# Attention with block sums and a squared-ReLU layer on one core: x moved by 128 bytes, the sums of w_out's blocks held back, and other constants in the planner

## Chip, cores and metric

The kernel runs on one core of a Trainium2 chip. The metric is the device time of one execution in microseconds (us). Four engines compute: TensorE (PE in the profile; PEld is its loading of stationary operands), VectorE (DVE), ScalarE (ACT) and GpSimd (POOL). SyncE (SP) issues every DMA of this kernel.

## The reference

```python
k_sum = k.reshape(B, H, nb, block, D).max(axis=3)      # B=4, H=8, S=768, D=64, block=32
v_sum = v.reshape(B, H, nb, block, D).mean(axis=3)
scores_l = scale * q @ k.T            # kept where |i - j| < 16
scores_s = scale * q @ k_sum.T + log(block)
a = softmax(concat([scores_l masked, scores_s]))
attn = a @ concat([v, v_sum])
x = attn as [3072 tokens, 512]
h = x @ w_in                          # [512, 2048]
g = relu(h) ** 2
out = g @ w_out                       # [2048, 512]
```

All of it is float32. TensorE multiplies it in a split form: each operand is taken as a high and a low part, and three products (high by high, low by high, high by low) are added.

## The kernel before

**Work.** The attention goes in 48 groups of 64 queries, the layer in units of 512 tokens, each unit in 16 items (a block of 128 columns of w_in, and the 128 rows of w_out that go with it). `xh` and `xl` hold the high and the low part of x for two units at a time. A first matmul of an item (`hidden`, line 1018 in the first two units, line 1305 in the others) is 12 matmuls of 512 columns: for each of four blocks of 128 inputs, w high with xh, w low with xh and w high with xl, all added in one bank of PSUM. A second one (line 1042) has 12 matmuls with w_out as the moving operand. In the four later units the second product is formed with fewer multiplications, from sums and differences of blocks of w_out (`combine`) and of g (`products`, line 1419: six matmuls each, gh or gl moving), and a part of the last two units' first products likewise from sums of x (`mixed`, line 1610; its x operands lie in `xh`, `xl`, in the room of `kb`, as xkb, and in tiles xs, xa, xgh, xgl).

**Order.** The order on each engine isn't written out. Every step is a task with an engine, a cost, a key (its due time), the tasks that it comes after and the buffers that it takes and uses; `Plan.order` plays the tasks through with those costs and writes the instructions in the order that comes out. Where several tasks of an engine are ready, the smallest key goes first; `begin` is a time ahead of which a task isn't started, `behind` a task that must have been started, `late` time added to a DMA's landing. A DMA lands, for the planner, its bytes at 350 GB/s and 1.9 us after its issue. A first matmul group costs 2.73 us there, a second one 12 times 0.2268 us.

**Buffers.** Tile `t` has three slots of 4,096 bytes. A conversion of a weight block (`convert`: loads L952, ACT L955 which takes a `t`, DVE L958 and L964, ACT L969, DVE L972) holds one of them from L955 to L972; a combine (`combine`: POOL L1111 twice, POOL L1126 four times, ACT L1129, DVE L1132, two stores L1136) takes two of them, cr and cs, ahead of L1111 and holds them until its stores have landed. Block sums of v (`batch_v`, loads L529, matmuls L539) take three for a batch after the second. The probabilities go through memory: VectorE's transpose L815 makes `a`, four stores L826 (tasks TW) and a load back L832 (TR) turn it, and the matmuls L842 (`values`, in `visit`) need it.

**Layout.** Tiles lie one behind another in the order in which the code makes them. The constants' pool begins at byte 1,152 of each partition, behind 1,024 bytes of scratch (asked for in `kernel`) and four constants of 32 bytes each. `ident` takes 512 bytes, so that `xh` begins at 1,664, which is 6 times 256 and 128; `xl` is 16,384 bytes on. `kb` follows behind all constants, at 47,488, which again is 128 past a multiple of 256. The weights w, and `t`, `r`, `gh`, `gl` and `a` begin at multiples of 256.

Of the kernel before, what the change touches and what calls it, by code (L numbers as in the profile page):

```python
# [10 lines left out]
F32 = mybir.dt.float32  # L11
# [9 lines left out]
P = 128  # L21
# [5 lines left out]
LINE = 256  # L27
# [3 lines left out]
TU = UG * TQ  # L31
# [18 lines left out]
FV_LEAD = 0  # L50
FV1_LEAD = 17.0
HALVED = 2
Q_LEAD = 23
XS_LEAD = 7
R_LEAD = 1
TR_LEAD = 18
WITH_ITEM = 0, 0, 1, 1, 0, 1, 0, 0, 0, 1, 0, 0, 1, 1, 1, 1
# [3 lines left out]
X_LEAD = 0  # L61
KEEPS = 20
GH_LEAD = 9
# [174 lines left out]
def attention_then_relu2_ffn(  # L238
# [95 lines left out]
    FIRST_STEP = 3.27, 2.88  # L334
    MIXED_STEP = 1.66
    X_BY = 40
    SUMS = 231.1, 245.7, 260.4, 275.0
    PRODUCT_STEP = 1.48, 1.58, 1.40
# [38 lines left out]
    ident = cst.tile([P, P], F32, name="ident")  # L377
    kb = sb.tile([P, NPAIR, NB + S], F32, tag="kb", name="kb", bufs=1)
# [39 lines left out]
    scratch = cst.tile([P, LINE // 16], F32, name="scratch")  # L418
    kinds["nm"] = Slots(None, "nm", 3, [cst.tile([P, LINE // 16], F32, name=f"nm{i}") for i in range(3)])
# [64 lines left out]
    means = const([P, S // P * NB], "means")  # L484

# [202 lines left out]
    def softmax(g, by_pe=False):  # L688
# [122 lines left out]
        else:  # L811
# [21 lines left out]

            t_w = add(f"TW{g}", "SP", 1.75, store, due - 8.5 - TR_LEAD, [t_T[g]], take=[d], use=[a], size=4 * P * DM)
            t_A[g] = add(f"TR{g}", "SP", 0.35, fetch, due - 8 - TR_LEAD, [t_w], use=[a, d], size=4 * P * DM)

# [83 lines left out]
    w_parts = {}  # L920

    def convert(f, ns):
# [59 lines left out]
        t2 = add(f"WM{name}", "ACT", 0.02 + 0.5 * k, rebias, due - 8, t1, take=[t], use=[raw])  # L982
        t3 = add(f"WR{name}", "DVE", 0.09 + 0.27 * k, rest, due - 8, t1, use=[raw])
# [119 lines left out]
    def combine(p):  # L1103

        due = unit_at[0] + 75 + 13.5 * p + LATER * (p > 5)
# [41 lines left out]
        for k in range(2):  # L1147
            t1.append(add(
                f"RC{p}_{k}", "POOL", 1.3, lambda k=k: whole(k), due + 1.3 * k, t_W[1, 2 * p + k],
                take=[raw, sums] * (not k), use=[raw] * k + ws[k], begin=due, behind=t1[0] if k else None,  # L1150
            ))
# [89 lines left out]
    def host(u, f):  # L1241
# [5 lines left out]
        if f in VIA_RING:  # L1247
# [4 lines left out]
            for k in range(2):  # L1252
# [3 lines left out]
                    due - 12 + 0.1 * k, [t_WI[f], *old], take=[xs[k]], size=4 * P * DM, begin=due - 30, behind=last_of("wc", None),  # L1256
# [83 lines left out]
    def products(s, todo):  # L1340
# [29 lines left out]
        for j, p, due in todo:  # L1370
# [19 lines left out]
                due - 12, t_WC[j, p], take=[chunk], size=4 * P * DM, begin=due - 25, behind=last_of("wc", None),  # L1390
# [71 lines left out]
    def sum_x():  # L1462
# [13 lines left out]
        def halves(x, k0=0):  # L1476
            return [Part(x, (2 * k0 + k) * TU, (2 * k0 + k + 1) * TU) for k in range(2)]
# [379 lines left out]
```

## Time and profile before

| | us |
|---|---|
| median of three runs | 600.3 (599.33 to 601.23) |
| the profiled execution | 604.56 |
| its span, first to last instruction | 602.7 |
| PE busy in it | 585.3 |
| DVE, ACT, POOL busy | 415.9, 342.2, 96.6 |

The times are device times; the profiled execution lasts 1.9 us longer than the span that its instructions fill. A row of a timeline gives start, duration, engine, line, operation and tiles, and in brackets the idle time of the engine ahead of it with what ended that. A matmul's row lasts longer than its turn, since matmuls overlap: the time that one takes from the engine is the distance from its start to the next one's.

### The profile page before, as it was taken

How to read it: one execution, taken by the hardware profiler on the slowest of the kernel's cores; microseconds unless marked ns; L12 is line 12 of the kernel's file. 1: busy time of each engine (PE TensorE's matmuls, PEld its weight loads, DVE VectorE, ACT ScalarE, POOL GpSimd, SP SyncE). 2: the span in 40 equal slices, each digit the busy share in tenths (PEclk: the TensorE clock that was granted, in tenths of full speed). 3: DMA queues.
4: the chain of work that ended last, by engine and by line, in shares of the span. 5: the costliest groups of instructions: out<-in, count | busy, mean ns of one | idle time of the engine just before them, and what ended most of it. 6: DMA issues, size and time to landing. Idle time of an engine off the chain costs nothing.

```text
span 602.7 us, 11842 instructions
## 1 busy us (share of the span) xinstructions
PE 585.3 (97%) x4108; PEld 473.5 (79%) x4108; DVE 415.9 (69%) x942; ACT 342.2 (57%) x848; POOL 96.6 (16%) x141
## 2 busy tenths in 40 slices
PE   8889999989999999999989999999999999999996
PEld 6678878768887888888877888888888878788885
DVE  5999897666544615655975867798754945678764
ACT  2899687566654535564864566645643544454442
POOL 4400005263450016264300000000000000000000
PEclk9999999989999999999999999999999999999999
DMA  8999964977994757966998765878976144567672
GB/s 312 294 386 327 346 247 156 299 253 234 380 326 152 237 197 230 358 221 231 283 306 283 227 185 179 278 226 239 312 216 191 35 145 151 161 194 226 193 228 100
DMA packets 100958, 143.83 MB, mean 239 GB/s; under 512 B 10060, under 2 KB 55116, under 8 KB 100900
## 3 DMA queue, kind: packets, MB, share of 16 engines
q1 hardware_dynamic: 100900, 143.09, 73.3%
q8 instruction: 32, 0.52, 0.4%
q14 instruction: 26, 0.21, 0.1%
HBM read 102.42 MB, written 39.85 MB: 236 GB/s over the span
## 4 chain that ended last, share of the span: by engine, by line
PE 82%; DMA 7%; DVE 5%; ACT 2%; issue 2%; SPq 1%; DVEq 0%
PE o L1419 25%; PE h L1305 22%; PE o L1042 10%; PE h L1018 9%; PE o L1610 4%; PE x L842 3%; PE att L638 2%; DMA a<-turn 2%; PE sz L1610 2%; PE o L638 1%; DVE t L964 1%; DMA q<-qW 1%; DMA kb<-kT 1%; PE att L1610 1%; DMA v<-vS 1%
## 5 line engine op out<-in xcount | busy, mean ns | idle before, releaser
L1419 PE MATMUL o<-gh,w 128*128 128x512 f32 x448 | 121.0, 391 | 0.0
L1401 ACT CAST gh<-g 128x512 fp32r<-128x512 f32 x112 | 68.5, 621 | 60.9 <-PE o L1419 29.2
L1305 PE MATMUL h<-xh,w 128*128 128x512 f32 x320 | 100.7, 396 | 0.0
L1419 PEld LDWEIGHTS o<-gh,w 128*128 128x128 f32 x448 | 83.6, 188 | 17.8
L1406 DVE TENSOR_TENSOR gl<-g,gh 128x512 fp32r<-128x512 f32 x112 | 77.7, 706 | 24.0 <-ACT gh L1401 23.3
L1018 PE MATMUL h<-xh,w 128*128 128x512 f32 x240 | 76.9, 400 | 1.7 <-DVE w L972 1.0
L1305 PEld LDWEIGHTS h<-xh,w 128*128 128x128 f32 x320 | 59.8, 188 | 14.1
L1315 ACT ACTIVATE r<-h 128x512 f32<-128x512 f32 x48 | 28.5, 596 | 73.8 <-PE h L1305 72.9
L1419 PE MATMUL o<-gl,w 128*128 128x512 f32 x224 | 69.2, 389 | 0.0
L1305 PE MATMUL h<-xl,w 128*128 128x512 f32 x160 | 63.2, 395 | 0.0
L767 ACT ACTIVATE p<-p,nm 128x118 f32<-128x118 f32 x160 | 61.2, 388 | 2.5 <-DVE nm L712 2.5
L1042 PE MATMUL o<-w,gh 128*128 128x512 f32 x240 | 62.5, 396 | 0.0
L1018 PEld LDWEIGHTS h<-xh,w 128*128 128x128 f32 x240 | 45.3, 190 | 13.3 <-DVE w L972 1.7
L1042 PEld LDWEIGHTS o<-w,gh 128*128 128x128 f32 x240 | 44.9, 190 | 10.4
L1419 PEld LDWEIGHTS o<-gl,w 128*128 128x128 f32 x224 | 42.0, 188 | 9.0
L1018 PE MATMUL h<-xl,w 128*128 128x512 f32 x120 | 47.9, 400 | 0.0
L1032 DVE TENSOR_TENSOR gl<-r,gh 128x512 fp32r<-128x512 f32 x30 | 22.9, 764 | 33.6 <-PE o L1042 21.8
L712 DVE CUSTOM_DVE_ANT_0 p<-att,mask 128x118 f32<-128x118 f32 x152 | 32.9, 274 | 13.6 <-PE att L638 13.5
L651 POOL COPY kb<-kb 128x96 f32<-128x96 f32 x25 | 11.0, 440 | 181.2 <-ACT kw L663 60.4
L1111 POOL TENSOR_TENSOR cr<-w 128x512 f32<-128x512 f32 x16 | 26.4, 1666 | 73.3 <-PE vps L539 41.5
L1027 ACT ACTIVATE r<-h 128x512 f32<-128x512 f32 x30 | 17.9, 597 | 32.5 <-PE h L1018 32.5
L1305 PEld LDWEIGHTS h<-xl,w 128*128 128x128 f32 x160 | 30.1, 188 | 7.2
(200 smaller groups left out, 998.4 us busy)
## 6 DMA issues: line engine op xcount, KB each, us to landing
raw<-wW SPq DMA_DIRECT2D x32, 512.0 KB, 7.6
w<-scr_s SPq DMA_DIRECT2D x64, 256.0 KB, 2.8
w<-scr_a SPq DMA_DIRECT2D x48, 256.0 KB, 3.3
turn<-a SPq DMA_DIRECT2D x160, 64.0 KB, 2.6
a<-turn SPq DMA_DIRECT2D x40, 256.0 KB, 4.7
w<-scr_i SPq DMA_DIRECT2D x40, 256.0 KB, 5.5
v<-vS SPq DMA_DIRECT2D x33, 192.0 KB, 6.1
kb<-kT SPq DMA_DIRECT2D x16, 384.0 KB
```

The source lines that it names most:

```text
L712: nc.vector.tensor_tensor_reduce(out=pr.tile[:, j, :KEYS], in0=score_at(g, 0, j), in1=mask_of(g)[0], scale=-SCALE, scalar=-NEG, op0=ALU.ad ...
L767: nc.scalar.activation(x, score_tile(g, p % parts)[:, p] if by_pe else x, AF.Exp, bias=nm.tile[:, p : p + 1], scale=SCALE if by_pe else -1 ...
L1018: nc.tensor.matmul(cut(h), lhsT=lhs.tile[:, k * P : (k + 1) * P], rhs=rhs[:, k, c0 : c0 + n], start=(i == 0), stop=(i == 3 * KT - 1),)
L1032: lambda: nc.vector.tensor_tensor(out=cut(gl), in0=cut(r), in1=cut(gh).bitcast(F32), op=ALU.subtract),
L1042: nc.tensor.matmul(o_of(o, t), lhsT=terms[i][0].tile[:, (t - t0) * P : (t - t0 + 1) * P], rhs=terms[i][1].tile, start=(first and i == 0), ...
L1111: nc.gpsimd.tensor_tensor(out=raw.tile[:, k * DM : (k + 1) * DM], in0=ws[k][0].tile.bitcast(F32), in1=ws[k][1].tile.bitcast(F32), op=ALU.add)
L1305: nc.tensor.matmul(h.tile, lhsT=lhs.tile[:, k * P : (k + 1) * P], rhs=rhs[:, k, c0 : c0 + TU], start=(i == 0), stop=(i == 3 * KT - 1),)
L1315: t2 = add(f"RL{name}", "ACT", 0.56, lambda: nc.scalar.activation(r.tile, h.tile, AF.Relu), due + 2 - R_LEAD, [t1], take=[r], use=[h])
L1401: f"GH{s}_{n}", "ACT", 0.54, lambda x=x, gh=gh: nc.scalar.copy(out=gh.tile, in_=x.tile), due - GH_LEAD, ready,
L1406: lambda x=x, gh=gh, gl=gl: nc.vector.tensor_tensor(out=gl.tile, in0=x.tile, in1=gh.tile.bitcast(F32), op=ALU.subtract),
L1419: nc.tensor.matmul(o.tile[:, d], lhsT=chunk.tile[:, w * HALF + d * P : w * HALF + (d + 1) * P], rhs=y.tile, start=begins and w == 0 and y ...
L1610: nc.tensor.matmul(o.tile, lhsT=lhs(w, k), rhs=y[k], start=begins and i == 0, stop=i == 5, skip_group_check=not begins,)
```

## The change

Seven things change; everything else stays.

1. `scratch` and one of the three small `nm` tiles (64 bytes each) are made ahead of `xh`, the other two behind `means`. So `xh` begins at 1,792, `xl` 16,384 on, both multiples of 256; what lies behind `means` stays where it was, `kb` too. The three x operands in `kb`'s room start 32 elements (128 bytes) later, at multiples of 256.
2. The first half of a combine's first sum (RC) is put behind `t_WM[-1]`, the ACT step L955 of the last weight conversion: it isn't started before that.
3. The planner adds time to landings: 0.3 us to the stores of probabilities (TW), 0.6 us to their loads back (TR) from group 8 on, 0.5 us to loads of w_in's and w_out's parts from memory (HL, CL, SL).
4. Due times of the combines: 72 + 14.5 p in place of 75 + 13.5 p from the first unit's start.
5. Keys: loads of block sums 5 us earlier, evacuations Q of the mixed stage 4 us later, sums of x 6 us earlier, ACT's steps behind a first matmul 2 us earlier, turning of probabilities 12 us later, xh and xl 3 us earlier, gh and gl of the products 9 us earlier.
6. Which items of the fourth unit a product follows (eight of sixteen in both).
7. Step lengths from which due times are worked out, the times of the combines of w_in, and `KEEPS` (of the three visits with block sums one keeps its buffers free of others, where two did).

```diff
-FV_LEAD = 0
+FV_LEAD = 5
-Q_LEAD = 23
-XS_LEAD = 7
-R_LEAD = 1
-TR_LEAD = 18
-WITH_ITEM = 0, 0, 1, 1, 0, 1, 0, 0, 0, 1, 0, 0, 1, 1, 1, 1
+FETCH_LATE = 0.6
+LATE_FROM = 8
+COMB0 = 72
+COMB1 = 14.5
+Q_LEAD = 19
+XS_LEAD = 13
+R_LEAD = 3
+TR_LEAD = 6
+WITH_ITEM = 0, 0, 0, 1, 0, 1, 0, 1, 0, 1, 0, 1, 0, 1, 1, 1
-X_LEAD = 0
-KEEPS = 20
-GH_LEAD = 9
+X_LEAD = 3
+KEEPS = 30
+GH_LEAD = 18
...
-    FIRST_STEP = 3.27, 2.88
-    MIXED_STEP = 1.66
-    X_BY = 40
-    SUMS = 231.1, 245.7, 260.4, 275.0
-    PRODUCT_STEP = 1.48, 1.58, 1.40
+    FIRST_STEP = 3.20, 3.37
+    MIXED_STEP = 1.62
+    X_BY = 35
+    SUMS = 243.1, 255.3, 267.5, 299.8
+    PRODUCT_STEP = 1.50, 1.45, 1.40
...
     ident = cst.tile([P, P], F32, name="ident")
+    scratch, *small = (cst.tile([P, LINE // 16], F32, name=f"small{i}") for i in range(2))
...
-    scratch = cst.tile([P, LINE // 16], F32, name="scratch")
-    kinds["nm"] = Slots(None, "nm", 3, [cst.tile([P, LINE // 16], F32, name=f"nm{i}") for i in range(3)])
+    kinds["nm"] = Slots(None, "nm", 3, small)
...
     means = const([P, S // P * NB], "means")
+    small += [cst.tile([P, LINE // 16], F32, name=f"small{i}") for i in range(2, 4)]
...
-            t_w = add(f"TW{g}", "SP", 1.75, store, due - 8.5 - TR_LEAD, [t_T[g]], take=[d], use=[a], size=4 * P * DM)
-            t_A[g] = add(f"TR{g}", "SP", 0.35, fetch, due - 8 - TR_LEAD, [t_w], use=[a, d], size=4 * P * DM)
+            t_w = add(f"TW{g}", "SP", 1.75, store, due - 8.5 - TR_LEAD, [t_T[g]], take=[d], use=[a], size=4 * P * DM, late=0.3)
+            t_A[g] = add(f"TR{g}", "SP", 0.35, fetch, due - 8 - TR_LEAD, [t_w], use=[a, d], size=4 * P * DM, late=FETCH_LATE * (g >= LATE_FROM))
...
         t2 = add(f"WM{name}", "ACT", 0.02 + 0.5 * k, rebias, due - 8, t1, take=[t], use=[raw])
+        t_WM.append(t2)
...
-        due = unit_at[0] + 75 + 13.5 * p + LATER * (p > 5)
+        due = unit_at[0] + COMB0 + COMB1 * p + LATER * (p > 5)
...
-                take=[raw, sums] * (not k), use=[raw] * k + ws[k], begin=due, behind=t1[0] if k else None,
+                take=[raw, sums] * (not k), use=[raw] * k + ws[k], begin=due, behind=t1[0] if k else t_WM[-1],
...
-        def halves(x, k0=0):
-            return [Part(x, (2 * k0 + k) * TU, (2 * k0 + k + 1) * TU) for k in range(2)]
+        def halves(x, k0=0, at=0):
+            return [Part(x, at + (2 * k0 + k) * TU, at + (2 * k0 + k + 1) * TU) for k in range(2)]
...
-            3: (halves(of_kb), halves(of_kb, 1)), 0: (halves(of_kb, 2), pairs["a"]), 2: (halves(slots[0]), pairs["gl"]),
+            3: (halves(of_kb, 0, LINE // 8), halves(of_kb, 1, LINE // 8)), 0: (halves(of_kb, 2, LINE // 8), pairs["a"]), 2: (halves(slots[0]), pairs["gl"]),
```

The loads HL, CL and SL get `late=0.5` in the same way, each at its `add`.

## Rows read from the trace of the kernel before

**Rows 1.** Page, part 1: busy time, share and instructions of each engine.

```profile
PE 585.3 (97%) x4108; PEld 473.5 (79%) x4108; DVE 415.9 (69%) x942; ACT 342.2 (57%) x848; POOL 96.6 (16%) x141
```

**Rows 2.** Busy time by stretch, first row the columns (PEclk: granted share of TensorE's clock).

```profile
core 0: us, PE busy (x) PEld busy (x) DVE busy (x) ACT busy (x) POOL busy (x), PEclk, DMA share, GB/s
...
127.00:134.00 7.00, 5.61 (x16) 4.28 (x17) 3.85 (x3) 3.66 (x6) 5.12 (x6) 0.76 0.94 326
130.00:133.00 3.00, 3.00 (x9) 2.39 (x8) 1.70 (x1) 0.03 (x1) 3.00 (x3) 0.52 0.95 347
```

**Rows 3.** Chain that ended last, in order of time: start, length, engine, line, count.

```profile
229.10 2.79 PE h L1018 x12
231.89 2.73 PE o L1042 x12
...
521.94 76.22 PE o L1419 x336
```

**Rows 4.** Timeline of PE in the mixed stage (start, duration, operation, count).

```profile
487.57 1.55 PE L1610 MATMUL o<-xkb,w 128*128 128x512 f32 x6
488.96 1.07 PE L1610 MATMUL o<-xs,w 128*128 128x512 f32 x4
489.87 0.39 PE L1610 MATMUL o<-xgh,w 128*128 128x512 f32 x1
```

**Rows 5.** Groups of PE's matmuls by line and shape: count, busy us, mean ns.

```profile
L1018 PE MATMUL h<-xh,w 128*128 128x512 f32 x240 | 76.9, 400 | 1.7 <-DVE w L972 1.0 <-ACT w L969 0.7
L1305 PE MATMUL h<-xh,w 128*128 128x512 f32 x320 | 100.7, 396 | 0.0
L1305 PE MATMUL h<-xh,host 128*128 128x512 f32 x64 | 20.1, 395 | 0.0
L1610 PE MATMUL o<-xkb,w 128*128 128x512 f32 x24 | 6.2, 394 | 0.0
```

**Rows 6.** Timeline of PE where it waits for the last weight conversion.

```profile
127.61 0.50 PE L1018 MATMUL h<-xh,w 128*128 128x512 f32 x1 [0.75 <-ACT w L969]
128.90 0.50 PE L1018 MATMUL h<-xh,w 128*128 128x512 f32 x1 [0.78 <-DVE w L972]
```

**Rows 7.** Timelines of DVE, ACT and POOL around the last conversion and the first combines.

```profile
113.35 0.68 DVE L958 TENSOR_SCALAR raw<-raw 128x1024 uint32<-128x1024 uint32 x1
114.53 1.23 DVE L972 TENSOR_TENSOR w<-t,w 128x1024 fp32r<-128x1024 f32 x1 [0.51 <-ACT w L969]
...
123.66 1.15 ACT L955 ACTIVATE t<-raw 128x1024 f32<-128x1024 f32 x1
...
92.37 3.51 POOL L1111 TENSOR_TENSOR cr<-w 128x512 f32<-128x512 f32 x2
...
115.84 3.92 POOL L1111 TENSOR_TENSOR cr<-w 128x512 f32<-128x512 f32 x2 [15.15 <-DVE w L972]
```

**Rows 8.** Timeline of PE: matmuls that wait for a load or an evacuation.

```profile
114.29 1.32 PE L842 MATMUL x<-a,v 118*64 118x64 f32 x32 [1.21 <-DMA a<-turn]
...
305.64 0.69 PE L842 MATMUL x<-a,v 118*64 118x64 f32 x16 [1.57 <-DMA w<-scr_a]
...
325.16 0.69 PE L842 MATMUL x<-a,v 118*64 118x64 f32 x16 [0.52 <-DMA a<-turn]
...
491.16 0.73 PE L1610 MATMUL o<-xs,w 128*128 128x512 f32 x2 [0.68 <-ACT g L1628]
```

**Rows 9.** Page, part 6: issues of one DMA, KB each, median us to landing.

```profile
a<-turn SPq DMA_DIRECT2D x40, 256.0 KB, 4.7
```

**Rows 10.** Timelines of POOL and SP, and the chain, ahead of the third batch's block sums.

```profile
168.90 1.74 POOL L1111 TENSOR_TENSOR cr<-w 128x512 f32<-128x512 f32 x1
...
187.67 0.45 SPq L1136 DMA_DIRECT2D scr_s<-cs  x1
...
210.61 2.33 SPq L529 DMA_DIRECT2D fv<-vS  x5
...
222.67 1.44 PE vps L539 x48
```

More of the change, by code (lines that the diff above doesn't have):

```diff
@@ L919, in attention_then_relu2_ffn @@
     t_W = {}
-    w_parts = {}
+    w_parts, t_WM = {}, []
     def convert(f, ns):
@@ L1255, in host @@
                     lambda k=k: nc.sync.dma_start(out=xs[k].tile.bitcast(F32), in_=scr_i[i][:, k * DM : (k + 1) * DM]),
-                    due - 12 + 0.1 * k, [t_WI[f], *old], take=[xs[k]], size=4 * P * DM, begin=due - 30, behind=last_of("wc", None),
+                    due - 12 + 0.1 * k, [t_WI[f], *old], take=[xs[k]], size=4 * P * DM, begin=due - 30, behind=last_of("wc", None), late=0.5,
                 ))
@@ L1389, in products @@
                 ),
-                due - 12, t_WC[j, p], take=[chunk], size=4 * P * DM, begin=due - 25, behind=last_of("wc", None),
+                due - 12, t_WC[j, p], take=[chunk], size=4 * P * DM, begin=due - 25, behind=last_of("wc", None), late=0.5,
             )
@@ L1590, in product @@
                     lambda: nc.sync.dma_start(out=chunk.tile.bitcast(F32), in_=scr_t[p][c].rearrange("p w x -> p (w x)")),
-                    due - 12, t_sums[0, p], take=[chunk], size=4 * P * DM, begin=due - 25, behind=last_of("wc", None),
+                    due - 12, t_sums[0, p], take=[chunk], size=4 * P * DM, begin=due - 25, behind=last_of("wc", None), late=0.5,
                 )]
```

## The prediction, made before the changed kernel ran

> **What bounds the kernel now.** I read the page's busy times first. PE is busy for 585.3 of a span of 602.7 us, far ahead of VectorE's 415.9 [rows 1]. So there are two ways to shorten the time: shorten the matmuls, or take away the moments at which PE waits. A busy matmul's row says nothing of its cost, because rows overlap; the chain of waits gives whole groups one behind another, and there a group's length divided by its count is the cost of one. A first matmul group of 12, with x moving, lasts 2.79 us, which is 232.5 ns each; the group behind it, with w_out moving, lasts 2.73 us, 227.5 ns each; 336 products at the end, with gh and gl moving, last 76.22 us, 226.8 ns each [rows 3]. All are 128 by 128 by 512 in float32. The reader should see that the matmuls that read x cost 5 to 6 ns more than the others. For the waits I read PE's own timeline: two in the first units at 127.6 and 128.9 us for the last conversion of weights [rows 6], behind which the granted clock is down to 0.52 from 130 to 133 us, that is at the lower of its two levels (1.2 instead of 2.4 GHz) for nearly all of that stretch [rows 2]; three of the matmuls that need fetched probabilities, and short ones in the mixed stage [rows 8].
>
> **1. x at a multiple of 256 bytes.** Is the address the cause of the 5 to 6 ns? The mixed stage tells. There, on one line of code, with the same kind of stationary operand and six matmuls into one bank as for every other group there, six matmuls moving xkb (128 bytes past a multiple of 256) take 488.96 - 487.57 = 1.39 us, 231.7 ns each; the next four, moving xs (at a multiple of 256), take 489.87 - 488.96 = 0.91 us, 227.5 ns each [rows 4]. So neither the line nor the single bank costs the difference; of what I can tell from the layout, the address is left. The matmuls that the change moves to a multiple of 256: 240 on line 1018 with xh and half as many with xl, 360; 320 and 64 with xh on line 1305 and half as many with xl, 576; on line 1610 the 24 shown and 16 more with xkb, and 72 with xh and xl, 112; together 1,048 of 512 columns [rows 5], and 48 of 256 columns that I leave out. At 233 - 227.3, about 5.7 ns each, that is 6.0 us. Ends: if a stream that has been disturbed by the small matmuls of a visit stays at 229.5 ns (halfway), 1,048 x 3.2 = 3.4 us; if all run at the 226.8 ns of the last stretch, and the second groups lose their last 0.7 ns over 360 too, 1,048 x 6.2 + 0.3 = 6.8 us. PE is the bound, so it counts in full. VectorE and ScalarE write x at the new place; a loss there has their idle time, 31% and 43% of the span, to hide in [rows 1]. A side effect: the planner's cost of a first group is 2.73 us, against the measured 2.79; with the cost come true, the chip falls less behind the plan.
>
> The Trainium skill, "SBUF — State Buffer", section "Specifications (TRN2)", speaks against this term: SBUF is read in lines of 16 bytes, and two hits in each line give full bandwidth. Both addresses are multiples of 16 and the reads are contiguous, so by that rule alone the move would bring nothing, and the sum below would end at 597.2 us. The trace's 231.7 against 227.5 ns is against that.
>
> **2. First combine behind the last conversion.** The raw weights of the last conversion had landed by 113.35 us, when VectorE's first step ran on them; the ACT step that needs a `t` ran only at 123.66 us. Between lay the first combine, which had taken two of the three `t` at 92.37 us, and the second, which began at 115.84 us [rows 7]. With the combine held back, conversion 15 follows conversion 14, whose last step runs from 114.53 to 115.76 us [rows 7], some 3 us behind, at about 119 us. PE wants it at 126.7 us, so there are 7 us of room. Gone then: the 0.75 us of idle time ahead of 127.61; of the 1.29 us from there to 128.90 all but one turn, 1.06 us [rows 6]; and the slow clock: from 130 to 133 us the profile counts 9 matmuls where at 233 ns there is room for 12.9 [rows 2], with the slow ones on either side (0.76 over the seven microseconds) about 8.5 turns at some 430 ns, 8.5 x 0.2 = 1.7 us. Sum 3.5 us. Ends: 0, if another holder of `t` takes the place; 3.5. I take 3.5, since a load that is there 10 us early is the nearest row. The clock needs no own cause: it fell behind the two waits. What the wait added for POOL holds up: POOL goes in order, and behind RC lie the copies of kb (L651) and the later combines. All combines slide by about one place, 115.84 - 92.37 = 23 us at first. Their results are wanted by the products from 291 us on, so that costs nothing while the slots last (rival 3).
>
> **3. Longer times for fetches.** The planner reckons 0.35 + 262,144 / 350,000 + 1.9 = 3.0 us from issue to landing of a load back of probabilities; the trace has a median of 4.7 [rows 9]. It puts the visit too early, and PE stands still: 1.21 us at 114.29, 1.57 at 305.64 and 0.52 at 325.16 [rows 8], 3.3 us together. The second row names a weight fetch (w<-scr_a), which these matmuls don't read, so I take the load back that they do read for its cause. The added 0.6 is a third of the 1.7 that the plan is short by, and 0.3 and 0.5 on stores and on weight loads push in the same direction. I take half, 1.6 us; ends 0 and 3.3. Against it works that the turning's key is 12 us later, so that its four stores and its load go behind other loads on SP's queue; the plan sees that and puts the visit later still, so I count nothing.
>
> **4. All other constants** change which ready task goes first. They add no work. The trace has no row for them; the bounds are the waits of this kind that stand in the old order: the mixed stage's 0.7 us at 491.16 [rows 8], of which there are two, 1.4 us, may go, and as many as all waits of parts 2 and 3, 3.5 + 3.3 = 6.8 us, could come anew in other places. A new order seldom comes without some; nearest is the size of the waits for single loads and evacuations in the rows, 0.5 to 1.6 us, so I put two of them, 2.0 us more, with -1.4 and +6.8 as ends. In all three stages with a combine, a load or an evacuation under PE's work the other engines have room: GH 9 us earlier and the first sums of x 6 us earlier make ACT and DVE work ahead, and would cost only if a slot of gh is then held by a later product than the one that PE wants.
>
> **Sum.** On the profiled execution: 604.56 - 6.0 - 3.5 - 1.6 + 2.0 = 595.5 us (the span to about 593.6). The runs' median lies 4.3 us below the profiled time, so the median comes to 600.3 - 9.1 = 591.2 us.
>
> **Rivals.** (1) The reordering gives nothing back: new waits for fetches and evacuations eat parts 2 and 3, while x's matmuls do get faster. For it: the constants were moved in both directions at once, and PE's waits change place with any new order. Against: the stall at 127 us has one clear cause, which the change takes away. 600.3 - 6.0 = 594.3, and up to 597.5 where they take 3 us more than they give. (2) The change to the address does nothing, the difference belonging to what x's matmuls do and not to where x lies. Against: rows 4. Then 600.3 - 3.1 = 597.2. (3) Slower: the `t` slots. Before, the second to the sixth combine began (168.90 - 115.84) / 4 = 13.3 us apart, the sixth stored at 187.67, and the block sums' loads, which need all three slots, went at 209.6 to 212.9 for matmuls at 222.67 [rows 7, 10]. With the first combine in the second's place the sixth stores at 187.7 + 13.3 = 201 us. That leaves 8.6 us to the loads, and 222.67 - 212.94 - 4.7 = 5.0 us more from the landing of the last (a load of 256 KB takes 4.7 [rows 9]) to the matmuls. If the combines take 13 us more than that in all, or one more of them gets its two slots ahead of the loads, the visit waits for a combine: 13.3, and 4.7 for the load, less the 5.0 to spare, 13.0 us: 600.3 - 9.1 + 13.0 = 604.2. It decides at a store of the sixth combine later than about 214 us. Against it: the loads' keys are 5 us earlier. (4) Nearly all waits go, also those of the mixed stage: 600.3 - 6.8 - 3.5 - 3.3 - 1.4 = 585.3.
>
> **How the numbers follow.** The forecast (587 to 594) 0.55; rival 1 0.26; rival 2 0.07; rival 3 0.06; rival 4 0.06. The range: from the forecast's 591.2 down by the better end of parts 1 and 3 (0.8 and 1.7) and the waits that I added (2.0), 586.7, rounded to 586.5; up through rivals 1 and 2 to 597.5; beyond are rival 3, most of rival 4 and a rest of the others, under 0.2. A measurement of this kernel tells about 0.3%, 1.8 us, from no change. Faster by more: forecast, rivals 1 and 4, and most of 2: 0.88. Within: 0.06, the ends of rivals 1 to 3. Slower: 0.06, rival 3.
>
> **What would show it.** Part 1: groups h of 12 in the chain at 2.72 to 2.75 us instead of 2.79, and xkb's six at 1.36 to 1.37; if they stay at 2.79, rival 2. Part 2: ACT's L955 for the last time ahead of 120 us, POOL's first L1111 behind it, no wait for L969 or L972 around 127, and a granted clock of 1.00 there. Part 3: fewer or shorter waits of PE for a<-turn; none of the three over 0.7 us. Part 4: the sum of PE's waits behind 31 us, and new names among them. Rival 3: L539 in the third batch waiting for fv<-vS. Wrong would make the prediction above all a new wait of several microseconds with another fall of the clock behind it, at a place where the old order had none.

## Result, and the profile after

| | before | changed |
|---|---|---|
| median of the runs taken side by side, us | 601.23 (599.27 to 604.92, seven) | 594.12 (592.18 to 597.99, seven) |
| ratio | | 0.988, interval 0.9843 to 0.9916 |
| the profiled execution, us | 604.56 | 597.28 |
| its span, us | 602.7 | 595.1 |
| PE busy, us | 585.3 | 578.7 |

The kernel became faster by 1.2%, in the interval by 0.8 to 1.6%: on the 600.3 us that the prediction started from, 7.2 us (5.0 to 9.4). The forecast was 9.1, inside that interval near its end; rival 1, 6.0 us or less, lies inside it too. So the time alone doesn't tell these two apart. The trace and the experiments do.

The page's first part shows where most of it is: of the 7.6 us by which the two profiled spans differ, PE has 6.6 us less to do with the same 4,108 matmuls. (The lines of code named here are numbered 5 or 6 higher in the changed kernel: h's L1018 is now L1024, L1305 is L1311, o's L1042 is L1048, L1419 is L1425, values' L842 is L847. The kernels of the experiments shift them by 1 to 8.)

```profile
PE 578.7 (97%) x4108; PEld 473.2 (80%) x4108; DVE 417.0 (70%) x942; ACT 342.3 (58%) x848; POOL 92.4 (16%) x141
```

The chain of waits (start, length, engine, line, count) answers [rows 3]:

```profile
125.19 2.74 PE h L1024 x12
127.94 2.72 PE o L1048 x12
...
246.72 10.88 PE h L1311 x48
...
514.36 76.17 PE o L1425 x336
```

A first group, with x moving, now lasts 2.72 to 2.74 us where it lasted 2.79; 48 of its matmuls take 10.88 us, 226.7 ns each, the same as the 336 products at the end. The difference between matmuls that read x and the others is gone. The timeline of PE in the mixed stage (start, duration, operation, count) answers [rows 4]:

```profile
480.56 1.52 PE L1616 MATMUL o<-xkb,w 128*128 128x512 f32 x6
481.92 1.07 PE L1616 MATMUL o<-xs,w 128*128 128x512 f32 x4
482.82 0.39 PE L1616 MATMUL o<-xgh,w 128*128 128x512 f32 x1
```

xkb's six take 1.36 us instead of 1.39. The four behind them, with xs, take 0.90 us. The kernel before has six such groups of xs that don't wait, and the prediction read the fastest of them, 0.91 us. Here is another, with the xkb ahead of it, in the kernel before:

```profile
498.23 1.56 PE L1610 MATMUL o<-xkb,w 128*128 128x512 f32 x6
499.63 1.09 PE L1610 MATMUL o<-xs,w 128*128 128x512 f32 x4
500.55 0.63 PE L1610 MATMUL o<-xgh,w 128*128 128x512 f32 x2
```

There xs's four take 0.92 us, 230 ns each, against xkb's 1.40 us, 233 ns each. The difference is still there, but smaller, and xs, whose own address the change leaves as it is, gained too: groups next to a slow one aren't quite free of it.

The stall at 127 us [rows 6] is gone too, and the slow clock behind it [rows 2]. The first row is the stretch of busy times that showed it (PE, PEld, DVE, ACT, POOL, then the granted clock, the DMA share and GB/s); the two others are a stretch that had nothing to show before:

```profile
core 0: us, PE busy (x) PEld busy (x) DVE busy (x) ACT busy (x) POOL busy (x), PEclk, DMA share, GB/s
127.00:134.00 7.00, 7.00 (x87) 5.66 (x86) 2.21 (x11) 3.10 (x8) 1.65 (x3) 1.00 1.00 333
420.00:424.00 4.00, 1.81 (x53) 1.47 (x46) 1.82 (x10) 0.24 (x2) 0.00 (x0) 1.00 1.03 387
424.00:429.00 5.00, 5.00 (x15) 3.94 (x16) 4.36 (x16) 4.70 (x20) 0.00 (x0) 0.66 0.60 191
```

In 420 to 424 us PE is idle for more than half of the time while the DMA engines are full, and behind that the clock falls to 0.66. PE's timeline names the matmul that waits there, and SP's timeline has the issue of the load that it reads:

```profile
420.39 0.69 PE L847 MATMUL x<-a,v 118*64 118x64 f32 x16
423.27 0.69 PE L847 MATMUL x<-a,v 118*64 118x64 f32 x16 [2.19 <-DMA w<-scr_i]
```

```profile
416.11 0.32 SPq L837 DMA_DIRECT2D a<-turn  x1
416.47 0.44 SPq L1364 DMA_DIRECT2D out<-c  x1
416.95 3.20 SPq L1261 DMA_DIRECT2D w<-scr_i  x4
```

The brackets name a weight load, w<-scr_i, which values doesn't read; what it reads is the load back of probabilities issued at 416.11, next to a store of 512 KB and four weight loads of 256 KB, and PE's matmul starts 7.2 us after that issue.

Over all of PE's stream behind 41.5 us, I added up by how much each start lay beyond its ordinary distance from the one before. Ordinary is the median distance for that pair of shapes in the same trace, and a start counts where it lies more than 0.15 us beyond it: as idle where PE had nothing to do, as slow clock where it was busy and the granted clock was low.

```
kernel                                       idle   slow clock   (us)
before                                        7.8      1.6
changed                                       6.4      1.4
e1  address alone                             4.9      1.6
e2  changed, address undone                   4.1      0.0
e5  address and "behind" alone               15.2      0.0
e6  address and due times alone              13.1      1.6
e7  address and longer fetches alone         13.6      1.8
e8  changed without longer fetches            5.3      0.0
e12 changed, combines' due times undone       9.3      1.6
```

So most of the old waits went, and new ones came: of 9.4 us there are 7.8 left. They are those of one profiled execution each, and good for places more than for size. e1 shows how far: it has the order of the kernel before on every engine, and 2.9 us less of idle time.

### The profile page after: what moved, and what is told of

The parts are those of the page before. It is cut to its first block, busy times and chain, and to the rows that moved or that the text cites. A ratio compares the mean times of both kernels' runs of the same rounds, so it can differ in the third digit from the quotient of the medians.

```text
span 595.1 us, 11819 instructions
## 1 busy us (share of the span) xinstructions
PE 578.7 (97%) x4108; PEld 473.2 (80%) x4108; DVE 417.0 (70%) x942; ACT 342.3 (58%) x848; POOL 92.4 (16%) x141
## 4 chain that ended last, share of the span: by engine, by line
PE 79%; DMA 10%; DVE 5%; SPq 2%; ACT 2%; issue 2%; DVEq 0%; ACTq 0%
PE o L1425 25%; PE h L1311 22%; PE o L1048 10%; PE h L1024 9%; DMA raw<-wW 4%; PE o L1616 4%; PE x L847 3%; PE att L643 3%; PE sz L1616 2%; DMA qvpa_lent<-vF 1%; DMA v<-vS 1%; DVE t L969 1%; DMA kb<-kT 1%; PE att L1616 1%; DMA w<-scr_i 1%
## 5 line engine op out<-in xcount | busy, mean ns | idle before, releaser
L1425 PE MATMUL o<-gh,w 128*128 128x512 f32 x448 | 121.7, 393 | 0.5 <-ACT gh L1407 0.5
L1311 PE MATMUL h<-xh,w 128*128 128x512 f32 x320 | 99.1, 391 | 0.0
L1425 PEld LDWEIGHTS o<-gh,w 128*128 128x128 f32 x448 | 84.3, 189 | 18.6 <-ACT gh L1407 0.9
L1412 DVE TENSOR_TENSOR gl<-g,gh 128x512 fp32r<-128x512 f32 x112 | 79.7, 725 | 23.2 <-ACT gh L1407 22.8
L1024 PE MATMUL h<-xh,w 128*128 128x512 f32 x240 | 74.2, 390 | 0.0
L1425 PE MATMUL o<-gl,w 128*128 128x512 f32 x224 | 69.9, 393 | 0.0
L1311 PEld LDWEIGHTS h<-xh,w 128*128 128x128 f32 x320 | 59.7, 188 | 12.5
L1311 PE MATMUL h<-xl,w 128*128 128x512 f32 x160 | 62.3, 389 | 0.0
L1048 PE MATMUL o<-w,gh 128*128 128x512 f32 x240 | 61.7, 393 | 0.0
L772 ACT ACTIVATE p<-p,small 128x118 f32<-128x118 f32 x160 | 60.9, 385 | 0.2 <-DVE small L717 0.2
L1024 PEld LDWEIGHTS h<-xh,w 128*128 128x128 f32 x240 | 44.9, 188 | 9.7 <-DVE w L977 0.2
L1048 PEld LDWEIGHTS o<-w,gh 128*128 128x128 f32 x240 | 44.5, 188 | 9.8 <-ACT os L1085 0.3
L1425 PEld LDWEIGHTS o<-gl,w 128*128 128x128 f32 x224 | 42.5, 190 | 9.0
L1024 PE MATMUL h<-xl,w 128*128 128x512 f32 x120 | 46.7, 389 | 0.0
L656 POOL COPY kb<-kb 128x96 f32<-128x96 f32 x25 | 9.2, 367 | 192.8 <-ACT kw L668 72.0
L1311 PEld LDWEIGHTS h<-xl,w 128*128 128x128 f32 x160 | 30.0, 188 | 6.3
L1048 PE MATMUL o<-w,gl 128*128 128x512 f32 x120 | 33.7, 390 | 0.6 <-DVE gl L1038 0.6
```

The lines of the kernel that those rows point to most:

```text
L772: nc.scalar.activation(x, score_tile(g, p % parts)[:, p] if by_pe else x, AF.Exp, bias=nm.tile[:, p : p + 1], scale=SCALE if by_pe else -1 ...
L1024: nc.tensor.matmul(cut(h), lhsT=lhs.tile[:, k * P : (k + 1) * P], rhs=rhs[:, k, c0 : c0 + n], start=(i == 0), stop=(i == 3 * KT - 1),)
L1048: nc.tensor.matmul(o_of(o, t), lhsT=terms[i][0].tile[:, (t - t0) * P : (t - t0 + 1) * P], rhs=terms[i][1].tile, start=(first and i == 0), ...
L1311: nc.tensor.matmul(h.tile, lhsT=lhs.tile[:, k * P : (k + 1) * P], rhs=rhs[:, k, c0 : c0 + TU], start=(i == 0), stop=(i == 3 * KT - 1),)
L1412: lambda x=x, gh=gh, gl=gl: nc.vector.tensor_tensor(out=gl.tile, in0=x.tile, in1=gh.tile.bitcast(F32), op=ALU.subtract),
L1425: nc.tensor.matmul(o.tile[:, d], lhsT=chunk.tile[:, w * HALF + d * P : w * HALF + (d + 1) * P], rhs=y.tile, start=begins and w == 0 and y ...
```

## Experiments

Each ratio is to the kernel before, run beside it. It is the ratio on record for the runs taken together, which isn't quite the quotient of the two medians (for e1 0.9884 against 595.2 / 601.45 = 0.9896). For the sums all are put on 600.3 us: (ratio - 1) x 600.3.

**e1, the address alone.** The kernel before with point 1 of the change only:

```diff
+    scratch, *small = (cst.tile([P, LINE // 16], F32, name=f"small{i}") for i in range(2))
...
+            3: (halves(of_kb, 0, LINE // 8), halves(of_kb, 1, LINE // 8)), 0: (halves(of_kb, 2, LINE // 8), pairs["a"]), 2: (halves(slots[0]), pairs["gl"]),
```

> The kernel before with part 1 alone: xh, xl and the x operands in kb's room at multiples of 256 bytes, every instruction in the order of before. If the address is the cause, first matmul groups of 12 last 2.72 us instead of 2.79, and the time falls by 6 us (5 to 7), with the old waits at 114, 127, 305 and 325 us still there. If the address does nothing (rival 2), the groups stay at 2.79 and the time within 1 us of before. If the changed kernel's gain lies in the new order, this run is at the time of before.

Measured: 595.2 us beside 601.45, ratio 0.9884 (0.9843 to 0.9925), 7.0 us on 600.3 (4.5 to 9.4). Its chain, and PE's timeline at the old stall:

```profile
43.42 2.72 PE h L1019 x12
46.14 2.72 PE o L1043 x12
...
247.63 10.88 PE h L1306 x48
...
510.50 76.20 PE o L1420 x336
```

```profile
123.48 0.49 PE L1019 MATMUL h<-xh,w 128*128 128x512 f32 x1 [0.78 <-ACT w L970]
124.76 0.50 PE L1019 MATMUL h<-xh,w 128*128 128x512 f32 x1 [0.78 <-DVE w L973]
```

The whole gain of the change is there with the old order, and with the old stall still in it. But not all of the old waits are there, as the expectation had it. The wait of 305.64 stands at 298.13, with 0.81 us. The matmuls that had waited at 114.29 and 325.16 [rows 8] don't wait at all:

```profile
110.14 1.30 PE L843 MATMUL x<-a,v 118*64 118x64 f32 x32
...
316.28 1.15 PE L843 MATMUL x<-a,v 118*64 118x64 f32 x32
```

The order didn't change and the times of fetches in the plan didn't either. So waits for these loads come and go without either; those for the conversion stayed.

**e2, the order alone.** The changed kernel with the address undone (the same lines taken out).

> The changed kernel with part 1 undone: x 128 bytes past a multiple of 256 as before, the changed order kept. If the address is the whole gain, it takes as long as the kernel before (within 2 us), 6 us more than the changed one. If the order gives half of the gain, it lies some 3.5 us under before. First groups at 2.79 us either way.

Measured: 599.25 us, ratio 0.9965 (0.9936 to 0.9993), 2.1 us (0.4 to 3.8). First groups are back at 2.79:

```profile
43.97 2.79 PE h L1023 x12
46.76 2.73 PE o L1047 x12
```

With e1's 7.0 and e2's 2.1 the two halves would make 9.1 us; together they make 7.2. The intervals are wide enough for that to be chance, but the trace has a candidate. The same two visit matmuls as at 420 us above, with all instructions in the same order, in e2's timelines of PE and SP:

```profile
423.54 0.69 PE L846 MATMUL x<-a,v 118*64 118x64 f32 x16
424.70 0.69 PE L846 MATMUL x<-a,v 118*64 118x64 f32 x16 [0.48 <-DMA a<-turn]
```

```profile
418.81 0.32 SPq L836 DMA_DIRECT2D a<-turn  x1
```

From the issue of the load to the first of the two matmuls lie 4.7 us in e2, 4.3 in the changed kernel; from the issue to the second, which needs it, 5.9 and 7.2. With faster matmuls PE comes to the visit a little earlier in the load's life, and the load took longer. The first half of that is the address: of the kernels below with this order up to there, e3, with slow products, comes 4.6 us after the issue and waits 0.64 us, while e4, e10 and e11 come after 3.9, 3.4 and 3.6 us and wait 1.83, 1.65 and 2.17. The second half is not of the kernel: from the issue to the second matmul lie 5.7 us in e10 and 6.4 in e11, with the same order, so the 7.2 belongs to one execution. What made that load slow no run shows.

**e3, the other operands off the boundary.** The changed kernel with 128 bytes of padding ahead of tile r, which puts r, gh, gl, a and kw 128 past a multiple of 256.

```diff
+            if s.tag == "r" and not s.made:
+                s.pool.tile([P, 32], F32, tag="pad", name="pad", bufs=1)
```

> The changed kernel with 128 unused bytes ahead of r, gh, gl, a and kw, so that these lie 128 past a multiple of 256; order unchanged. If it is the moving operand's address that counts, the 672 product matmuls (gh or gl moving) go from 226.8 to 233 ns, the 336 at the end from 76.2 to 78.3 us, the time rises by about 4 us, and the second groups of the first two units (gh, gl stationary there, w moving) stay at 2.72. If the stationary operand's address counts as well, those rise too. If only x is touched by this, nothing changes.

Measured: 600.54 us, ratio 0.9991 (0.9965 to 1.0018), which is 6.7 us above the changed kernel's. Its chain:

```profile
43.97 2.73 PE h L1026 x12
46.70 2.80 PE o L1050 x12
...
514.38 78.41 PE o L1427 x336
```

The products at the end, with gh and gl moving, now cost 78.41 / 336 = 233.4 ns each. So the effect follows the address to other tiles. And the second groups on L1050 rose from 2.72 to 2.80 us, though the operand that moves there is w, which lies where it lay: what lies at 128 is gh and gl as the stationary operand. So the address of the stationary operand counts as much as that of the moving one, which the expectation had only as its second case. The two add up to the measured time: 672 products at 6.7 ns more are 4.5 us, 30 second groups at 0.08 us are 2.4, together 6.9 beside 6.7.

**e4, half way.** x at 64 bytes past a multiple of 256 (three small tiles ahead of xh instead of two).

```diff
+    scratch, *small = (cst.tile([P, LINE // 16], F32, name=f"small{i}") for i in range(3))
```

> The changed kernel with xh and xl 64 bytes past a multiple of 256 instead of at one; the operands in kb's room as in the changed kernel; order unchanged. If reads are cut at multiples of 256 bytes, whatever the distance, first groups are at 2.79 us again and the time rises by 5 to 6 us. If a multiple of 64 is enough, nothing changes and the 128 of before would stay unexplained.

Measured: 599.03 us, ratio 0.9952 (0.9919 to 0.9985), 4.3 us above the changed kernel's. Its chain:

```profile
127.16 2.76 PE o L1048 x12
...
144.56 2.76 PE h L1024 x12
...
247.13 11.00 PE h L1311 x48
```

48 matmuls take 11.00 us, between the 10.88 of a multiple of 256 and the 11.14 to 11.20 that 48 took at 128 past one (before): 64 costs a little under half. The second group, o in the first row, has 2.76 as well, though none of its operands had moved. Its neighbours' x had, so a slow group slows the next one too; by what, no run shows.

The Trainium skill, "SBUF — State Buffer", section "Specifications (TRN2)", has lines of 16 bytes and full bandwidth with two hits in each. 0, 64 and 128 are all multiples of 16, and three different times were measured: the measurement decides, and for TensorE's operands in this kernel the place within 256 bytes matters.

**e5, "behind" with the address.** e1 with the combine's first half put behind t_WM[-1], old due times.

```diff
-                take=[raw, sums] * (not k), use=[raw] * k + ws[k], begin=due, behind=t1[0] if k else None,
+                take=[raw, sums] * (not k), use=[raw] * k + ws[k], begin=due, behind=t1[0] if k else t_WM[-1],
```

> The kernel before with x at multiples of 256 bytes and the first half of every combine's first sum behind the last conversion's ACT step, all other constants as before. In this plan the sum is really held back (in the changed kernel, with or without it, the order is the same). Theory: the two waits for w at 123 to 125 us and the slow clock behind them go, 3.5 us less than the kernel with x alone (595.2), about 592; POOL's first sum moves from 91 to beyond 105 us and nothing waits for it. Rival: the combines that come later hold the t slots against the block sums of the third batch, a new wait of PE at 215 to 235 us, and 595 or more.

Measured: 603.95 us, ratio 1.0044 (1.0016 to 1.0072): 9.6 us more than e1, where 3.5 less was expected. The stall for the conversion is gone, as intended, and PE waits in other places, none of them the one that the rival named:

```profile
136.14 0.69 PE L843 MATMUL x<-a,v 118*64 118x64 f32 x16 [2.18 <-DMA a<-turn]
...
385.83 0.72 PE L1421 MATMUL o<-gl,w 128*128 128x512 f32 x2 [1.63 <-DVE gl L1408]
...
457.47 1.21 PE L1612 MATMUL att<-xh,w 128*128 128x512 f32 x4 [1.80 <-DVE small L713]
```

**e6, the due times with the address.** e1 with 72 + 14.5 p for the combines.

```diff
-        due = unit_at[0] + 75 + 13.5 * p + LATER * (p > 5)
+        due = unit_at[0] + 72 + 14.5 * p + LATER * (p > 5)
```

> The kernel before with x at multiples of 256 bytes and only the combines' due times of the change (72 + 14.5 p instead of 75 + 13.5 p). In the program's order conversion 15 then comes ahead of conversion 14 and of the first combine. Theory: this is what took the wait at 127 us away in the changed kernel: no wait for w, the clock at 1.00 there, POOL's first sum still at 91 us, about 592 us. Rival: the wait is tied to something else of the change, and stays at 123 to 125 us: 595.

Measured: 603.4 us, ratio 1.0018 (0.9984 to 1.0052): 8.0 us more than e1. The theory holds for the stall, which is gone here as well, and not for the time. The first new wait stands 12 us ahead of where the stall was:

```profile
111.16 1.29 PE L843 MATMUL x<-a,v 118*64 118x64 f32 x32 [2.54 <-ACT t L956]
...
383.51 1.22 PE L1420 MATMUL o<-gl,w 128*128 128x512 f32 x2 [1.35 <-DVE gl L1407]
...
456.28 1.19 PE L1611 MATMUL att<-xh,w 128*128 128x512 f32 x4 [1.80 <-DVE small L713]
```

In the changed kernel the same visit runs at 111.99 us without a wait. The loads of the conversion and the load back of probabilities stand in the same order on SP's queue in both, and the load back is issued at 105.5 us there and 105.1 here; but here PE is at the visit at 111.16 - 2.54 = 108.6 us, 3.4 us earlier. So at this place the due time pays only together with a plan that puts the visit later. The other new waits, at 381 to 384 and at 456 us, are not explained by it.

**e7, longer fetches with the address.** e1 with the `late` times of point 3.

```diff
+            t_w = add(f"TW{g}", "SP", 1.75, store, due - 8.5 - TR_LEAD, [t_T[g]], take=[d], use=[a], size=4 * P * DM, late=0.3)
+            t_A[g] = add(f"TR{g}", "SP", 0.35, fetch, due - 8 - TR_LEAD, [t_w], use=[a, d], size=4 * P * DM, late=0.6 * (g >= 8))
...
```

> The kernel before with x at multiples of 256 bytes and only the longer times of fetches (0.3, 0.6, 0.5 us). Theory: PE's waits for the load back of probabilities behind group 10 (1 to 1.7 us in the kernels without it) fall under 0.7 us in sum, the wait for w at 123 stays; 594. Rival: the order that comes out has as many waits, in other places; 595 to 597.

Measured: 605.73 us, ratio 1.0084 (1.0055 to 1.0114): 12.0 us more than e1; the theory failed. The stall for the conversion stays, at 126.20 and 127.48 us, and three waits for a<-turn add up to 4.9 us, the longest at a place where e1 has none:

```profile
452.39 0.69 PE L843 MATMUL x<-a,v 118*64 118x64 f32 x16 [2.85 <-DMA a<-turn]
```

**e8, the change without longer fetches.** The changed kernel with every `late` at 0.

```diff
-FETCH_LATE = 0.6
+FETCH_LATE = 0.0
```

> The changed kernel without the longer times of fetches. Theory: the one long wait for a load back that the changed kernel has, 2.4 us at 423 us with the slow clock behind it, is not cured by 0.6 us; without them there are more such waits, the sum of PE's waits for a<-turn goes from 2.4 to 3.5 us or more, 595 to 597 us. Rival: they do nothing or harm, 592 to 594.

Measured: 595.4 us, ratio 0.9901 (0.987 to 0.9932). Beside the changed kernel's 0.988 that is no difference, and both the theory's 595 to 597 and the rival's 592 to 594 lie within the noise. Of a<-turn there is one wait of PE over half a microsecond behind 41.5 us, in another place than before or after:

```profile
172.51 0.69 PE L847 MATMUL x<-a,v 118*64 118x64 f32 x16 [1.77 <-DMA a<-turn]
```

**e9, are the new waits for gh and gl of e6 a matter of lead?** e6 with gh and gl of the products 9 us earlier, as in the change (`GH_LEAD` 18).

> x at multiples of 256 bytes, the combines' due times of the change, and of the other constants only the one that makes the products' gh and gl 9 us earlier. With due times alone the kernel took 603.4 us, and its longest new waits of PE are for gh and gl at 293, 381 and 384 us (3.8 us), for the attention's maxima at 456 (2.0) and for a conversion at 111 (2.7). Theory: gh and gl made earlier take away the waits at 293 to 384 us; about 599 to 600. Rival: those waits come from the moved fetches of the weights' sums and stay; 603.

Measured: 603.26 us, ratio 1.0037 (1.0017 to 1.0057). The waits of e6 at 380.96 and 383.51 us stand there still, at 383.32 with 1.01 us and at 385.83 with 1.31. The lead is not their cause; what is stays open.

**e10 and e11, the waits of the mixed stage.** The changed kernel with `AT_FIRST`, the number of the last unit's plain items that go between the first products of the mixed stage and the rest of them, at 2 and at 1 instead of 3.

> The changed kernel with two items ahead of the mixed stage's first product of summed x instead of three, so that one more item stands between later products. The order changes from 440 us on alone. Theory: one of PE's waits for the evacuation Q2 (0.84 us each at 484 and 507 us) goes, since an item of 2.7 us stands there; 0.8 us less than the changed kernel, 593.3. Rival: the sums of x are not ready that early, and PE waits 2 us and more for them; 595 or more.

> As the run with two items ahead, with one. Theory: both waits for Q2 go, and the 0.28 us at 513; 1.7 to 2 us less than the changed kernel, 592.3. Rival: the sums of x come too late for the first product that needs them, and the wait there costs more than both; 596 or more.

Measured: 596.31 and 596.65 us, ratios 0.9918 (0.9897 to 0.9938) and 0.9914 (0.9887 to 0.994). The changed kernel waits twice for g's evacuation, 0.68 us each at 484.11 and 506.85. e10 still has both, at 480.73 and 503.46, e11 as well, at 485.04 and 505.05, and each has one more of 0.87 ahead of them. In time neither differs from the changed kernel by more than the runs can tell. The theory that an item put ahead of these products takes the waits away falls.

**e12, the due times taken out of the change.** The changed kernel with 75 + 13.5 p, and without `behind`.

```diff
-COMB0 = 72
-COMB1 = 14.5
+COMB0 = 75
+COMB1 = 13.5
...
-                take=[raw, sums] * (not k), use=[raw] * k + ws[k], begin=due, behind=t1[0] if k else t_WM[-1],
+                take=[raw, sums] * (not k), use=[raw] * k + ws[k], begin=due, behind=t1[0] if k else None,
```

> The changed kernel with two of its constants undone: the combines' due times are 75 + 13.5 p again in place of 72 + 14.5 p, and the combine's first half is no longer put behind the last conversion. Everything else of the change stays, the address of x and the longer fetch times too. Theory (the due time alone moved conversion 15 ahead of conversion 14 and of the first combine): the first combine takes its two slots of t ahead of conversion 15 again, PE waits for L974 and L977 between 120 and 130 us, together 1.5 to 2.5 us, with a granted clock under 0.8 behind the waits in a stretch of some microseconds; about 3 us over the changed kernel, 596.5 to 598. Rival 1 (the wait costs only its place, since what PE loses there the plan would lose elsewhere): the waits at 120 to 130 us return, but others go, 594 to 596. Rival 2 (other constants of the change keep conversion 15 early): no wait for L974 or L977 over 0.5 us, 594 to 595.

Measured: 598.9 us beside 602.3, ratio 0.9953 (0.9922 to 0.9984): 4.4 us more than the changed kernel. The old stall is back, and ACT's step L960 of the last conversion is at 119.86 us:

```profile
119.86 1.14 ACT L960 ACTIVATE t<-raw 128x1024 f32<-128x1024 f32 x1
```

```profile
123.79 0.50 PE L1024 MATMUL h<-xh,w 128*128 128x512 f32 x1 [0.70 <-ACT w L974]
125.07 0.51 PE L1024 MATMUL h<-xh,w 128*128 128x512 f32 x1 [0.78 <-DVE w L977]
```

The theory holds in the order and in the place and price of the waits (0.9 + 1.05 us beyond the ordinary distance). In the clock it failed in this execution: behind the same two waits, which in e1 stand at 123.48 and 124.76, the clock fell in e1's profiled execution and not in e12's. First e1's row of the stretch, then e12's:

```profile
125.00:130.00 5.00, 5.00 (x16) 3.94 (x16) 2.32 (x2) 1.71 (x3) 4.32 (x4) 0.66 0.99 343
```

```profile
125.00:130.00 5.00, 4.93 (x22) 4.10 (x23) 2.79 (x4) 2.72 (x4) 4.15 (x3) 1.00 0.99 341
```

Other waits that the changed kernel doesn't have are 1.41 us for a<-turn at 173.22 and 0.49 at 110.64. The profiles don't account for the whole 4.4 us: the two spans lie 1.4 us apart (596.5 and 595.1). By the table above e12 has 3.1 us more of idle time and slow clock, and its first matmul of h starts 1.8 us earlier (43.19 against 45.02).

**The four corners.** All four with x at a multiple of 256; ratio to before, and the difference to e1 on 600.3 us:

| | other constants and longer fetches as before | as changed |
|---|---|---|
| combines due at 75 + 13.5 p | e1: 0.9884 | e12: 0.9953, 4.1 us slower |
| due at 72 + 14.5 p | e6: 1.0018, 8.0 us slower | changed: 0.988, 0.2 us faster |

Either half of the reorder alone makes the kernel slower (for e12 narrowly, since its interval and e1's just touch); both together bring it back to where the address alone had brought it.

## Why the prediction came out as it did

**Part 1, x at a multiple of 256: right in cause and size.** Predicted were 6.0 us (3.4 to 6.8). PE's busy time fell by 6.6; alone (e1) it brought 7.0, and 5.1 where the other order runs around it (changed against e2). Both signs named ahead were there: groups h at 2.72 to 2.74 and xkb's six at 1.36. The reading that carried it was a comparison inside one stage, the same line with two tiles at two addresses [rows 4]. It read the fastest of six such groups of xs; another one, above, has 233 against 230 ns, since its neighbours slow it. The conclusion doesn't hang on it any more: e1, e2, e3 and e4 each move an address alone and find the time that goes with it. What the prediction didn't see: it counted on the moving operand alone. e3 shows that the stationary one counts as well; since w, gh and gl lay on the boundary before, nothing in the sum depended on it. The "last 0.7 ns" of the second groups, put in the upper end, came true too, 2.73 to 2.72.

**Part 2, the first combine behind the last conversion: the wait went as forecast, the mechanism was wrong.** The wait and the slow clock of 3.5 us at 127 us are gone. That this was worth 3.5 us isn't shown: undone inside the changed plan (e12) the wait cost 1.9 us where it stands, and done alone (e6) it made the kernel slower. But POOL's first L1117 isn't behind the last conversion, as the prediction wanted to see. ACT's last two L960 and POOL's first sum, in the changed kernel's timelines:

```profile
104.22 1.18 ACT L960 ACTIVATE t<-raw 128x1024 f32<-128x1024 f32 x1 [4.29 <-DMA raw<-wW]
...
110.52 1.18 ACT L960 ACTIVATE t<-raw 128x1024 f32<-128x1024 f32 x1 [2.37 <-DMA raw<-wW]
```

```profile
90.76 3.51 POOL L1117 TENSOR_TENSOR cr<-w 128x512 f32<-128x512 f32 x2
```

`behind` orders the plan's starts; no instruction waits for it on the chip. With the other constants in place it orders nothing: the program has the same instructions in the same order on all five engines with it and without it. What moves the conversion is the due time, point 4, which the prediction had thrown in with "all other constants". Due 3 us earlier, the first combine takes its two slots of `t` sooner, the slot of conversion 11 is left to conversion 15 and then 14, and both are done by 115.3 us. e6 and e12 show it from both sides: with 72 the stall is gone, with 75 it is there. So the sentence "with the combine held back, conversion 15 follows conversion 14" is the step that failed: the combine was not held back at all, and conversion 15 went ahead of 14. The combines didn't slide by a place either, on which rival 3 hung, and PE has no wait for the block sums.

**"The clock needs no own cause: it fell behind the two waits"** is the second step that fell. It fell in the profiled executions of before and e1, and not in that of e12, behind two waits of the same length that stand 1.3 us apart. Nor does the kernel alone decide it. Each execution has its mean granted clock on record, and a stretch like that of before (0.76 over 7 us [rows 2]) lowers it by 0.003. Of 89 executions of the kernel before, 30 have 0.999 or 1.000, so no such stretch; their median is 600.1 us, and that of the 59 others 602.5. Of the seven of the changed kernel, three have 1.000. The profiled execution of before was one with the fall, at 604.56 us. The prediction took the 1.7 us of its slow clock, and its waits, off a median of 600.3 us, as if every execution had them.

**Part 3, longer fetches: the three waits are gone, but not shown to be gone by this, and the time is worth nothing.** None of the three old waits [rows 8] is over 0.7 us. But two of them are gone in e1 too, which has no longer fetches. The load back's median fell from 4.7 us [rows 9] to 4.3, and is 4.2 in e1 without them and 4.7 in e12 with them. A new wait of 2.2 us with 1.4 us of slow clock stands at 423 us, the sort of thing that the last sentence of the prediction named as what would make it wrong. Undone in the changed kernel (e8) the longer times are worth nothing that the runs can tell; alone (e7) they cost 12 us. The term of 1.6 came out near 0. It could not be read off, because a longer landing in the plan moves every task that is ordered by it, so what it does to three waits says little of what it does to the others.

**Part 4, all other constants: the term that was mis-sized.** It stood as +2.0, with -1.4 and +6.8 as ends, for whatever new waits would come. Taken as a whole, parts 2 to 4 were to bring 3.5 + 1.6 - 2.0 = 3.1 us. e2 gives 2.1 for them at the old address, and the changed kernel against e1 0.2, with x aligned. So by the medians of these ratios the time came out nearer to 7 than to 9 us; the intervals don't exclude the 3.1. The forecast had the right sign and, as to the time, can't be told from rival 1; in the traces it is rival 1 that happened: x's matmuls faster, and new waits for fetches that eat most of what the reorder took away. That the total still came near the forecast is part 1 and some luck: of the other three terms one was put on a step that didn't take place, one was worth nothing, and a lump for unknown waits happened to take 2.0 of their 5.1 us off again.

The table of four corners says what was wrong in the form of the sum. Its terms were taken to be independent, each costed at its own place in the old order. The due times are worth 4.4 us inside the changed plan and cost 8.0 outside it, a difference of 12 us in a change of 7. "They add no work" was true, and no help.

**Left open.** What makes gh and gl late at 380 to 386 us in e5, e6 and e9. By what means an operand's address slows TensorE, and a slow group its neighbour. Why the load back issued at 416.11 us was slow in that execution. How much of e2's 2.1 us is left with x aligned: its interval and that of the changed kernel against e1 overlap. No kernel of the series is faster than the changed one by more than the runs can tell; e1, with nothing but the address, equals it.

## What to carry to other kernels

Look at the addresses of both operands of a matmul stream, in one stage where two tiles at different offsets share a line: one part in forty of a matmul's time may lie in 128 bytes of padding, and this gain needs no new order. Cost a reorder as a whole, against rows of all the waits that stand and with an end on the other side, since here its pieces cost time alone; and try the smallest piece of a change alone before its other pieces are credited. Before a wait or a slow clock is priced, look for it in more than one execution: here some stood in both traces of one order, others in one of the two. Where a planner writes the order, ask of every constraint whether anything on the chip waits for it: a due time decided here what a "behind" was written to decide.

## What the runs showed of the hardware that was not expected

- **The stationary operand's address.** gh and gl at 128 past a multiple of 256 as stationary operands, with w moving on the boundary, cost 2.80 us for 12 instead of 2.72 (e3), as much as a moving operand there.
- **64 bytes cost a little under half of 128.** 48 matmuls took 10.88, 11.00 and 11.14 to 11.20 us at 0, 64 and 128 past a multiple of 256, and at 64 a neighbouring group without a moved operand took 2.76 instead of 2.72 (e4).
- **Equal waits, unequal clocks.** Two waits of about a microsecond, 1.3 us apart, had a granted clock of 0.66 behind them over five microseconds in e1's profiled execution and of 1.00 in e12's; one wait of 2.2 us at 423 us had 0.66 behind it in the changed kernel's.
- **One kernel, unequal clocks.** Executions of the kernel before had a mean granted clock from 0.990 to 1.000 over their spans; the 30 of 89 with 0.999 or more had a median of 600.1 us, the others 602.5.
- **One order, unequal waits.** With the same instructions in the same order, PE waited 1.21 us for a load in the kernel before and not at all in e1 (114.29 and 110.14 us).
